# Five small experts in four 32-column tiles, and a large one as 128 and 32 rows

## The chip, the cores and the metric

The kernel runs on one core of a Trainium2 chip. The metric is the device time of one execution in microseconds (us), taken as the median of several runs. A profiled execution of the same program, a run by itself, gives the trace from which all rows below come; its span is counted from its first to its last instruction.

## What is computed

Three layers follow one another: an attention with a narrow window and block sums, a layer of eight experts of which each token takes one or none, and a dense feed-forward layer. The expert layer and the layer behind it are what matters here:

```python
skip_score = x @ w_skip                      # x: 1536 tokens of 512 numbers
do_compute = skip_score > 0
...
logits = xc @ w_gate                         # xc: the tokens to compute
e_idx = np.argmax(logits, axis=1)            # one of 8 experts
...
for e in range(E):
    mask = e_idx == e
    h = np.maximum(xc[mask] @ w1[e], 0.0)    # w1[e]: 512 x 1024
    y[mask] = gate_w[mask, None] * (h @ w2[e])   # w2[e]: 1024 x 512
out[do_compute] = xc + y
...
h = x @ w_in                                 # feed-forward: 512 x 2048
g = np.where(pos, h, np.where(neg, 0.0, (h + beta) ** 2 / (4.0 * beta)))
return (g @ w_out)                           # 2048 x 512
```

All is float32. For the inputs drawn here 428 of the 1536 tokens go to an expert; the eight experts get 179, 131, 60, 23, 13, 10, 9 and 3 of them. Tokens that are skipped go straight to the feed-forward layer.

## The kernel before, in words

**Routing.** The attention is computed for 12 tiles of 128 tokens. Each tile's rows are scattered to a buffer in memory (`xf`), skipped tokens from the front and computed ones from the back, and the row numbers of each expert's tokens go into a list (`ids_d`). The kernel does not know at build time which expert is large. It sorts the experts by counts on VectorE and works on eight places p = 0 to 7. Place 0 is the expert that is largest after three tiles; its first 128 tokens are computed at the end of the attention (`fb_x` to `fb_b`). Places 1 to NEARLY - 1 are experts that have gained few tokens of late, chosen after seven tiles. The rest are sorted at the end, largest first, and `PLACES` says which of them comes at which place.

**Experts.** `experts` runs over the places in the order 0 to 7. A place has room for 64 tokens, and the one in `BIG` (place 4) for 64 and another 128. The row numbers are loaded by SyncE (SP) in `get_ids`, and the rows gathered by GpSimd (POOL) in `get_x`, into one of 7 buffers x (`xring`) in turn, so that a gather waits for the scatter of the buffer's former rows. For a place of 64 rows, `x64` turns the rows (4 transposes of TensorE, PE), `a64` multiplies them with w1 in two halves of 512 columns, `t64` turns the result h (4 transposes), `b64` multiplies with w2, and `y64` adds the result to the rows on VectorE (DVE) and scatters them (`put`). In `a64` and `b64` the 64 tokens are the stationary operand, so each matmul fills only 64 of the 128 columns of PE; the two halves f = 0 and 1 write to PSUM partitions 0 to 63 and 64 to 127 and stand side by side. A float32 matmul is two instructions in the trace, so `a64` and `b64` are 16 each.

**Order.** PE, ACT and DVE instructions of the expert and feed-forward stages are ordered by a scheduler at build time, with priorities; SP and POOL follow the written order. At place p stand, in this order: `t64(p)`, `y64(p-1)`, `a64(p+1)`, the turning of place p+2, `b64(p)`. Weights of a place are 4 MB in four transfers of 1 MB (`fetch(p, c)`, c = 0, 1 for w1 and 2, 3 for w2), into slots that place p shares with p+3: `fetch(p+3, 0)` waits until `a64(p)` has ended, `fetch(p+3, 2)` until `b64(p)` has. Behind the last of them SP issues two reads of rows for the feed-forward layer (`get_slots` 0 and 1), the raw weights of its steps f = 4 and 5 (2 MB), and two more reads of rows (2 and 3).

**Feed-forward.** `feed` takes 512 tokens at a time (ch = 0 to 2) and 16 steps f of 128 columns each. Its weights come as 64-bit raw data that DVE and ACT rebuild into two float32 parts (`ff_bits` in three steps, `ff_round`); the steps f = 0 to 3 and the turning of the first 512 tokens (`turn0`) are filled into the expert stage, so many at each point as `FILLS` says. The first matmul of a step is `mm1` (tile hf). In the order of PE the first `mm1` stands behind the last expert's `b64` and all of `turn0`.

Of the kernel before, what the change touches and what calls it, by code (L numbers as in the profile page):

```python
# [8 lines left out]
F32 = mybir.dt.float32  # L9
# [4 lines left out]
ALU = mybir.AluOpType  # L14
# [8 lines left out]
SENT = 1 << 20  # L23
EARLY = 512
NV = 6
NEARLY = 3
BIG = (4,)
EOFF = 28 * CAP
SLOTS = (("00", "01"), ("02", "03"), ("10", "11"))
FFSLOTS = ("12", "13", "10", "11", "00", "01", "02", "03")  # L30
NRAW = 4
FILLS = ((2, 1, 1), (2, 1, 1), (2, 1, 1), (2, 1, 1), (0, 0, 0, 0), (0, 0, 0), (2, 0, 0))
LAST = 2
FFILLS = ((2, 1, 2), (2, 0, 2))
SHIFT = {'bits': 6, 'round': -57, 'act': -1, 'add': -97, 'g': 8, 'y': 18, 'x': -8, 't': 6, 'turn': 0}
YLAST = 4
PLACES = {3: 2, 4: 0, 5: 3, 6: 1, 7: 4}


@with_exitstack  # L40
def tile_net(ctx, tc, q, k, v, w_skip, w_gate, w1, w2, w_in, w_out, out):
    nc = tc.nc
    w_in, w_out = w_in.bitcast(I32), w_out.bitcast(I32)
    B, H, S, D = q.shape
    E = w_gate.shape[1]
# [22 lines left out]
    ident = cp.tile([128, 128], F32, name="ident")  # L68
# [35 lines left out]
    wx = {}  # L104
    ereg = {}

    def room(p):

        return 192 if p in BIG else 64

    def fetch(p, c):

# [33 lines left out]
    def rows(p, off):  # L146

        return ereg[p] * CAP + off + (ereg["n"] if p == 0 else 0)
# [22 lines left out]
    st = {}  # L171
# [9 lines left out]
    def get(key, row, n):  # L181

        get_ids(key, row, n)
        get_x(key)

    def get_ids(key, row, n):
        ids = cp.tile([128, 1], I32, tag="ids", name="ids", bufs=10)
        load_ids(ids[0:n], row)
        st["ids", key] = ids, n
# [36 lines left out]
    def attention(actx):  # L226
        per = actx.enter_context(tc.tile_pool(name="at_per", bufs=1))
        wk = actx.enter_context(tc.tile_pool(name="at_wk", bufs=2))
        rt = actx.enter_context(tc.tile_pool(name="rt", bufs=2))
        ps = actx.enter_context(tc.tile_pool(name="at_ps", bufs=2, space=PSUM))  # L230
# [629 lines left out]
    def experts(mctx):  # L860
        st["wk"] = wk = mctx.enter_context(tc.tile_pool(name="mo_wk", bufs=2))
        st["ps"] = ps = mctx.enter_context(tc.tile_pool(name="mo_ps", bufs=2, space=PSUM))

        def put(key, n):
            ids, xg = st.pop(("x", key))
            apart(scatter(ids[0:n], xg[0:n]), xg)


        def x64(key):
            xg = st["x", key][1]  # L870
            tp = ps.tile([128, 4, 64], F32, tag="tp", name="tpx", bufs=3)
            for kk in range(4):
                nc.tensor.transpose(tp[:, kk], xg[0:64, 128 * kk:128 * kk + 128], ident[0:64, 0:64])
            st["xT", key] = xT = wk.tile([128, 4, 64], F32, tag="xT", name="xT", bufs=3)
            with shift("x"):
                nc.scalar.copy(out=xT, in_=tp)  # L876

        def a64(key, p):
            xT = st["xT", key]
# [5 lines left out]
            st["h", key] = h = wk.tile([128, 512], F32, tag="h", name="h", bufs=2)  # L885
            nc.scalar.activation(out=h, in_=hp, func=AF.Relu)

        def t64(key):
            tp = turned(st.pop(("h", key)), ps.tile([128, 4, 128], F32, tag="tp", name="tph", bufs=3))
            st["hT", key] = hT = wk.tile([128, 4, 128], F32, tag="hT", name="hT", bufs=3)  # L890
            with shift("t"):
                nc.scalar.copy(out=hT, in_=tp)  # L892

        def b64(key, p):
            hT = st.pop(("hT", key))
# [7 lines left out]
        def y64(key):  # L903
            xg = st["x", key][1]
            yp = st.pop(("y", key))
            with shift("y"):
                for a in (0, 64):
                    nc.vector.scalar_tensor_tensor(out=xg[0:64, 0:512], in0=yp[a:a + 64], scalar=xg[0:64, 512:513],  # L908
                                                   in1=xg[0:64, 0:512], op0=ALU.mult, op1=ALU.add)
            put(key, 64)  # L910

        def mx(key):
            st["xT", key] = xT = wk.tile([128, 4, 128], F32, tag="xT", name="xTm", bufs=3)
            nc.scalar.copy(out=xT, in_=turned(st["x", key][1], ps.tile([128, 4, 128], F32, tag="tp", name="tpx", bufs=3)))

        def ma(key, p, f):
            if f == 0:
                t = wk.tile([128, 1024], F32, tag="h", name="hm")
                st["h", key] = t[:, 0:512], t[:, 512:1024]
            a128(p, st["xT", key], st["h", key], ps.tile([128, 512], F32, tag="h", name="hp", bufs=3), f)  # L920

        def mt(key):
            st["hT", key] = hT = wk.tile([128, 8, 128], F32, tag="hT", name="hTm", bufs=3)
            h = st.pop(("h", key))
            for a in range(2):
                t128(h, hT, ps.tile([128, 4, 128], F32, tag="tp", name="tph", bufs=3), a)

        def mb(key, p):
# [22 lines left out]
        x64(0)  # L951
        a64(0, 0)
        fetch(3, 0), fetch(3, 1)
        x64(1)
        st.pop("beyond")()
        for p in more:
            for key, off, m in more[p]:
                get_ids(key, rows(key[0] if m == 128 else key, off), m)
        for p in range(E - 1):
            last = p + 2 == E  # L960
            t64(p)
            if p in BIG:
                mt((p, 1))
            if p:
                y64(p - 1)
                if p - 1 in BIG:
                    put((p - 1, 1), 128)
            for key, off, m in more.get(p, ()):
                get_x(key)
            n = iter(FILLS[p])  # L970
            fill(next(n))
            a64(p + 1, p + 1)
            fill(next(n))
            if p + 1 in BIG:
                for f in range(2):
                    ma((p + 1, 1), p + 1, f)
            if p + 4 < E:
                fetch(p + 4, 0), fetch(p + 4, 1)
            for f in early[p]:
                f()  # L980
            if not last:
                x64(p + 2)
                if p + 2 in BIG:
                    mx((p + 2, 1))
            b64(p, p)
            if last:
                y64(p)
                t64(p + 1)
# [10 lines left out]
        b64(E - 1, E - 1)  # L999
        st["ylast"] = lambda: y64(E - 1)  # L1000
        fill(LAST)


# [294 lines left out]
```

## Time and profile before

| | us |
|---|---|
| median of 3 runs | 526.07 (525.96 to 526.61) |
| profiled execution, its time | 523.97 |
| profiled execution, its span | 521.9 |
| busy in the span: PE, DVE, ACT, POOL | 481.4, 271.6, 219.1, 94.7 |
| first instruction of the expert stage on PE | 149.88 |
| first `mm1` of the feed-forward stage | 241.10 |

The profiled execution is 2.1 us shorter than the median of the others, and its own time holds 2.1 us around the span. A difference found in the span is carried to the median as it stands. In the rows below, a line such as "160.07 3.65 PE L883 MATMUL hp<-w,xT ... x16" reads: at 160.07 us from the start of the span, for 3.65 us until the end of the last one, 16 matmuls of line 883 that write tile hp from tiles w and xT; "[1.67 <-ACT xh L205]" says that the engine stood idle for 1.67 us before it, until ACT's instruction of line 205 had ended. PEld is the loading of the stationary operand.

### The profile page before, as it was taken

What the parts mean: (1) busy time and instruction counts of PE and PEld (TensorE: products, weight loads), DVE (VectorE), ACT (ScalarE), POOL (GpSimd) and SP (SyncE); (2) the same over time, 40 slices, a digit from 0 to 9 for tenths busy, and PEclk for the clock granted to TensorE, in tenths of its full rate; (3) what the DMA queues carried; (4) which work ended last, traced back from release to release, by engine and by line L of the source; (5) the groups of instructions that cost most, each with busy time, mean ns of one, the idle gap of its engine ahead of it and who ended that gap; (6) DMA issues with size and microseconds to landing.
All of it is one profiled execution on the core that took longest, in us unless ns stands there. A gap on an engine that the chain in (4) does not pass through costs nothing.

```text
span 521.9 us, 7327 instructions
## 1 busy us (share of the span) xinstructions
PE 481.4 (92%) x2614; PEld 350.9 (67%) x2614; DVE 271.6 (52%) x612; ACT 219.1 (42%) x430; POOL 94.7 (18%) x167
## 2 busy tenths in 40 slices
PE   6887989973969999998999999999999999999994
PEld 3676979962423333435788888888888888888883
DVE  6665686972363421139899953433434453333341
ACT  6475637640112212122877666533324342333341
POOL 8505514505250310104000000020000011000002
PEclk9898989995879999998999999999999999999999
DMA  8997999989958999583654800020000001000002
GB/s 207 238 215 162 191 127 225 217 256 353 349 167 276 396 385 396 179 326 100 214 182 162 306 1 0 24 80 1 0 1 1 0 21 60 1 1 1 0 0 87
DMA packets 67981, 77.10 MB, mean 148 GB/s; under 512 B 32270, under 2 KB 49710, under 8 KB 67552
## 3 DMA queue, kind: packets, MB, share of 16 engines
q1 hardware_dynamic: 64480, 68.29, 45.7%
q0 software_dynamic: 3456, 8.26, 4.5%
q8 instruction: 22, 0.36, 0.3%
q14 instruction: 23, 0.19, 0.1%
HBM read 69.85 MB, written 8.12 MB: 149 GB/s over the span
## 4 chain that ended last, share of the span: by engine, by line
PE 45%; issue 34%; DVE 8%; ACT 5%; DMA 5%; POOL 1%; POOLq 0%; DVEq 0%; ACTq 0%
PE hf L1078 8%; PE hp L883 6%; PE yp L900 6%; DMA ids_d<-slot,si 3%; PE o L1119 3%; PE s L387 3%; PE o L1121 3%; PE o L1120 3%; PE hp L210 2%; PE lp L445 2%; PE xo L416 1%; POOL out_dram L1131 1%; PE yp L221 1%; DMA x<-xf,ids 1%; ACT p L392 1%
## 5 line engine op out<-in xcount | busy, mean ns | idle before, releaser
L1078 PE MATMUL hf<-xh,ffw 128*128 128x512 f32 x384 | 128.3, 396 | 1.7 <-ACT xh L205 1.7
L1078 PEld LDWEIGHTS hf<-xh,ffw 128*128 128x128 f32 x384 | 72.7, 189 | 18.3 <-ACT xh L205 1.9
L1119 PE MATMUL o<-ffw,g 128*128 128x512 f32 x192 | 76.8, 400 | 1.1 <-ACT g L1103 1.1
L1078 PE MATMUL hf<-xl,ffw 128*128 128x512 f32 x192 | 75.6, 394 | 0.4 <-DVE xl L206 0.4
L1120 PE MATMUL o<-ffw,g 128*128 128x512 f32 x192 | 75.9, 395 | 0.0
L1121 PE MATMUL o<-ffw,g 128*128 128x512 f32 x192 | 75.1, 395 | 0.0
L1131 POOL DMA_INDIRECT out_dram<-ob,perm x12 | 11.7, 974 | 257.5 <-DVE ob L1130 165.1
L1088 ACT ACTIVATE c<-c,scal 128x512 f32<-128x512 f32 x32 | 23.2, 724 | 76.7 <-DVE c L1087 76.6
L1098 DVE TENSOR_TENSOR hf<-hf,c 128x512 f32<-128x512 f32 x48 | 33.5, 698 | 41.1 <-ACT hf L1096 37.4
L1104 DVE TENSOR_TENSOR g<-hf,g 128x512 fp32r<-128x512 f32 x48 | 33.1, 689 | 24.6 <-ACT g L1103 24.6
L1087 DVE TENSOR_SCALAR c<-hf 128x512 f32<-128x512 f32 x32 | 22.1, 691 | 42.6 <-PE hf L1078 42.6
L1078 PEld LDWEIGHTS hf<-xl,ffw 128*128 128x128 f32 x192 | 36.5, 190 | 9.2 <-DVE xl L206 0.8
L1119 PEld LDWEIGHTS o<-ffw,g 128*128 128x128 f32 x192 | 36.1, 188 | 9.4 <-ACT g L1103 1.5
L1121 PEld LDWEIGHTS o<-ffw,g 128*128 128x128 f32 x192 | 36.2, 189 | 8.6
L1120 PEld LDWEIGHTS o<-ffw,g 128*128 128x128 f32 x192 | 36.3, 189 | 8.0
L392 ACT ACTIVATE p<-s,nm 128x120 f32<-128x120 f32 x96 | 26.7, 361 | 31.6 <-DVE nm L389 21.4
L1103 ACT CAST g<-hf 128x512 fp32r<-128x512 f32 x48 | 28.1, 586 | 28.1 <-DVE hf L1098 28.0
L883 PE MATMUL hp<-w,xT 128*64 128x512 f32 x128 | 32.0, 646 | 1.2 <-ACT xT L876 1.2
L908 DVE SCALAR_TENSOR_TENSOR x<-yp,x 64x512 f32<-64x512 f32 x16 | 12.0, 748 | 40.6 <-PE yp L900 33.0
L900 PE MATMUL yp<-w,hT 128*64 128x512 f32 x128 | 30.2, 599 | 0.7 <-ACT hT L892 0.7
L387 PE MATMUL s<-pb 128*128 128x120 f32 x192 | 27.3, 287 | 3.0 <-ACT pb L357 1.8
L387 PEld LDWEIGHTS s<-pb 128*128 128x128 f32 x192 | 27.2, 203 | 4.2 <-ACT pb L357 1.9
(203 smaller groups left out, 689.3 us busy)
## 6 DMA issues: line engine op xcount, KB each, us to landing
w<-in_moe_w_dram SPq DMA_DIRECT2D x32, 1024.0 KB, 10.9
raw<-in_moe_w_in_dram SPq DMA_DIRECT2D x16, 512.0 KB, 7.1
raw<-in_moe_w_out_dram SPq DMA_DIRECT2D x16, 512.0 KB, 4.6
x<-xf SPq DMA_DIRECT2D x12, 264.0 KB, 5.7
raw<-in_k_dram SPq DMA_DIRECT2D x16, 192.0 KB
raw<-in_q_dram SPq DMA_DIRECT2D x16, 192.0 KB, 4.4
vraw<-in_v_dram SPq DMA_DIRECT2D x4, 768.0 KB, 6.8
vw<-in_v_dram SPq DMA_DIRECT2D x13, 192.0 KB, 5.7
```

Of the source, the lines that this page charges most:

```text
L387: nc.tensor.matmul(s[:, u], tq[:, j], tk[:, j], start=False, stop=u == 3)
L392: nc.scalar.activation(out=p[:, u], in_=s[:, u], func=AF.Exp, bias=nm[:, u:u + 1], scale=1.0)
L883: nc.tensor.matmul(hp[64 * f:64 * f + 64], xT[:, kk], wx[p, 0][:, kk, 512 * f:512 * f + 512], start=kk == 0, stop=kk == 3)
L900: nc.tensor.matmul(yp[a], hT[:, kk, a], wx[p, 1][:, 4 * f + kk], start=kk == 0, stop=kk == 3)
L1078: nc.tensor.matmul(hp, w[:, 128 * kk:128 * kk + 128], a[:, kk], start=(n == 0), stop=(n == 11))
L1088: nc.scalar.activation(out=c, in_=c, func=AF.Square, bias=half, scale=0.5)
L1098: nc.vector.tensor_tensor(out=hp, in0=hp, in1=c, op=ALU.add)
L1103: nc.scalar.copy(out=gh, in_=hp)
L1104: nc.vector.tensor_tensor(out=gl, in0=hp, in1=gh.bitcast(F32), op=ALU.subtract)
L1119: nc.tensor.matmul(ops[ch][t], gh[:, a], hi, start=(f == 0), stop=False)
L1120: nc.tensor.matmul(ops[ch][t], gh[:, a], lo, start=False, stop=False)
L1121: nc.tensor.matmul(ops[ch][t], gl[:, a], hi, start=False, stop=(f == NF - 1))
```

## The change

Every place has a room of its own now: 64 rows at places 0 and 6, 32 rows at places 1, 2, 3, 5 and 7, and 160 at place 4, as 128 and 32. A place of n rows uses 128 / n tiles of n columns side by side (`sides`): for 32 rows four tiles, each with 256 columns of w1 in `as_`, and a quarter of w2's rows in `bs`; so h of 32 rows is 128 x 256, and two transposes turn it. `ys` adds the parts one by one: four additions for 32 rows, where 64 rows take two. One place more (3) is chosen early. Of the large expert, the part of 128 rows is gathered first and the part of 32 rows later; before, the part of 64 came first and that of 128 later.

```diff
-NEARLY = 3
+NEARLY = 4
 BIG = (4,)
+ROOM = (64, 32, 32, 32, 160, 32, 64, 32)
-FILLS = ((2, 1, 1), (2, 1, 1), (2, 1, 1), (2, 1, 1), (0, 0, 0, 0), (0, 0, 0), (2, 0, 0))
+FILLS = ((2, 1, 1), (1, 1, 0), (1, 1, 0), (1, 2, 1), (1, 1, 1, 1), (0, 0, 0), (2, 0, 0))
-PLACES = {3: 2, 4: 0, 5: 3, 6: 1, 7: 4}
+PLACES = {4: 0, 5: 2, 6: 1, 7: 3}
...
+    def tail(p):
+
+        return (128, ROOM[p] - 128) if p in BIG else (0, ROOM[p])
...
         for p in range(NEARLY):
-            get(p, rows(p, 0), 64)
+            get(p, rows(p, 0), room(p))
         late_regs()
-        get(3, rows(3, 0), 64)
         fb_b()
         fetch(2, 2), fetch(2, 3)
-        get(4, rows(4, 0), 64)
+        get((4, 1), rows(4, 0), 128)
...
+        def sides(n):
+
+            return [slice(n * i, n * i + n) for i in range(128 // n)]
...
-            hp = ps.tile([128, 512], F32, tag="h", name="hp", bufs=3)
+            n = st["n", key]
+            xT, m = st["xT", key], 8 * n
+            hp = ps.tile([128, m], F32, tag="h", name="hp", bufs=3)
             for kk in range(4):
-                for f in range(2):
-                    nc.tensor.matmul(hp[64 * f:64 * f + 64], xT[:, kk], wx[p, 0][:, kk, 512 * f:512 * f + 512],
-                                     start=kk == 0, stop=kk == 3)
+                for f, a in enumerate(sides(n)):
+                    nc.tensor.matmul(hp[a], xT[:, kk], wx[p, 0][:, kk, m * f:m * f + m], start=kk == 0, stop=kk == 3)
...
-            for kk in range(4):
-                for f in range(2):
-                    a = slice(64 * f, 64 * f + 64)
-                    nc.tensor.matmul(yp[a], hT[:, kk, a], wx[p, 1][:, 4 * f + kk], start=kk == 0, stop=kk == 3)
+            for c in range(n // 16):
+                for f, a in enumerate(sides(n)):
+                    nc.tensor.matmul(yp[a], hT[:, c, a], wx[p, 1][:, n // 16 * f + c], start=c == 0, stop=c == n // 16 - 1)
...
-                for a in (0, 64):
-                    nc.vector.scalar_tensor_tensor(out=xg[0:64, 0:512], in0=yp[a:a + 64], scalar=xg[0:64, 512:513],
-                                                   in1=xg[0:64, 0:512], op0=ALU.mult, op1=ALU.add)
-            put(key, 64)
+                for a in sides(n):
+                    nc.vector.scalar_tensor_tensor(out=xg[0:n, 0:512], in0=yp[a], scalar=xg[0:n, 512:513],
+                                                   in1=xg[0:n, 0:512], op0=ALU.mult, op1=ALU.add)
+            put(key, n)
...
-        more = {0: (((4, 1), 64, 128), (5, 0, 64)), 1: ((6, 0, 64),), 3: ((7, 0, 64),)}
+        more = {0: (4, 5), 1: (6,), 3: (7,)}
```

On PE, from the transposes of place 2 to those of place 4, before (x_71 and x_72 hold the rows of places 2 and 3, x_73 and x_74 the two parts of place 4; the order counts a float32 matmul once):

```order
L873 MATMUL tpx<-ident,x_71 128x64 x4
L900 MATMUL yp<-w_1372,hT 64x512 x8
L200 MATMUL tph<-ident,h 128x128 x4
L883 MATMUL hp<-w_1938,xT 64x512 x8
L873 MATMUL tpx<-ident,x_72 128x64 x4
L900 MATMUL yp<-w_1899,hT 64x512 x8
L200 MATMUL tph<-ident,h 128x128 x4
L883 MATMUL hp<-w_2215,xT 64x512 x8
L873 MATMUL tpx<-ident,x_73 128x64 x4
L200 MATMUL tpx<-ident,x_74 128x128 x4
L900 MATMUL yp<-w_2176,hT 64x512 x8
```

and the same stretch of PE now:

```order
L881 MATMUL tpx<-ident,x_71 128x32 x4
L910 MATMUL yp<-w_1372,hT 64x512 x8
L900 MATMUL tph<-ident,h 128x128 x2
L892 MATMUL hp<-w_1948,xT 32x256 x16
L881 MATMUL tpx<-ident,x_72 128x32 x4
L910 MATMUL yp<-w_1909,hT 32x512 x8
L900 MATMUL tph<-ident,h 128x128 x2
L892 MATMUL hp<-w_2215,xT 32x256 x16
L881 MATMUL tpx<-ident,x_74 128x32 x4
L205 MATMUL tpx<-ident,x_73 128x128 x4
L910 MATMUL yp<-w_2176,hT 32x512 x8
```

The steps stand in the same order; only their shapes and counts differ, and the small part of place 4 is still turned ahead of the 128 rows, though it lies in the other buffer now.

On POOL, the gathers from the fourth on, before (xf<-x_73 is the scatter of the first 128 tokens, xf<-x_76 that of place 0):

```order
L163 DMA x_72<-xf,ids 64x528
L168 DMA xf<-x_73,ids_1654 1536x528
L163 DMA x_73<-xf,ids 64x528
L163 DMA x_74<-xf,ids 128x528
L163 DMA x_75<-xf,ids 64x528
L168 DMA xf<-x_76,ids 1536x528
```

and now:

```order
L168 DMA x_72<-xf,ids 32x528
L173 DMA xf<-x_73,ids_1654 1536x528
L168 DMA x_73<-xf,ids 128x528
L168 DMA x_74<-xf,ids 32x528
L168 DMA x_75<-xf,ids 32x528
L173 DMA xf<-x_76,ids 1536x528
```

The 128 rows of place 4 have taken the fifth place, and its small part the sixth.

## Rows read from the trace of the kernel before

**Rows 1.** The page: span, and busy time of each engine.

```profile
span 521.9 us, 7327 instructions
PE 481.4 (92%) x2614; PEld 350.9 (67%) x2614; DVE 271.6 (52%) x612; ACT 219.1 (42%) x430; POOL 94.7 (18%) x167
```

**Rows 2.** Timeline of PE, 100 to 250 us: one place, the large one, the end.

```profile
160.07 3.65 PE L883 MATMUL hp<-w,xT 128*64 128x512 f32 x16
163.66 0.46 PE L873 MATMUL tpx<-ident,x 64*128 64x64 f32 x4
164.04 3.65 PE L900 MATMUL yp<-w,hT 128*64 128x512 f32 x16
167.63 0.66 PE L200 MATMUL tph<-ident,h 128*128 128x128 f32 x4
168.22 3.65 PE L883 MATMUL hp<-w,xT 128*64 128x512 f32 x16
...
179.95 0.46 PE L873 MATMUL tpx<-ident,x 64*128 64x64 f32 x4
...
208.73 7.13 PE L221 MATMUL yp<-w,hTm 128*128 128x512 f32 x16
...
234.75 3.65 PE L900 MATMUL yp<-w,hT 128*64 128x512 f32 x16 [0.67 <-ACT hT L892]
238.34 1.09 PE L200 MATMUL tps<-ident,x 128*128 128x128 f32 x8
241.10 0.96 PE L1078 MATMUL hf<-xh,ffw 128*128 128x512 f32 x3 [1.67 <-ACT xh L205]
```

**Rows 3.** Waits of PE from 160 to 239 us (total, times, longest).

```profile
PE yp L900 <- ACT hT L892: 0.7, 1, 0.7
```

**Rows 4.** Windows: busy of each engine, granted clock, DMA share, GB/s.

```profile
160.00:210.00 50.00, 50.00 (x229) 18.82 (x228) 15.65 (x18) 11.87 (x22) 8.12 (x9) 1.00 1.03 380
210.00:222.00 12.00, 12.00 (x48) 4.81 (x48) 1.13 (x2) 1.45 (x3) 1.90 (x2) 1.00 0.53 161
222.00:232.00 10.00, 10.00 (x50) 3.79 (x48) 2.81 (x6) 2.26 (x4) 0.91 (x1) 1.00 1.05 385
232.00:234.00 2.00, 2.00 (x10) 0.69 (x6) 0.75 (x2) 0.00 (x0) 0.00 (x0) 1.00 0.44 161
```

**Rows 5.** Timeline of SP, 215 to 240 us: the last weights and the rows.

```profile
215.90 0.95 SPq L118 DMA_DIRECT2D w<-in_moe_w_dram  x2
...
225.26 1.90 SPq L852 DMA_DIRECT2D x<-xf  x2
```

**Rows 6.** Single weight transfers issued at 168.57 and 195.84 us, to landing.

```profile
w<-in_moe_w_dram SPq DMA_DIRECT2D x1, 1024.0 KB, 11.3
w<-in_moe_w_dram SPq DMA_DIRECT2D x1, 1024.0 KB, 8.7
```

**Rows 7.** Timeline of PEld near 104 us: stationary loads of 64 columns, attention.

```profile
103.59 0.60 PEld L416 LDWEIGHTS xo<-pb,pts 120*64 120x64 f32 x16
```

**Rows 8.** Timeline of POOL, 142 to 246 us: the sixth gather of expert rows.

```profile
169.50 1.03 POOL L163 DMA_INDIRECT x<-xf,ids  x1 [9.11 <-DMA ids<-ids_d]
```

**Rows 9.** Its issue: KB (none known), us to landing.

```profile
x<-xf,ids POOLq DMA_INDIRECT x1, 6.5
```

**Rows 10.** Timeline of ACT ahead of the first `mm1`.

```profile
239.03 0.58 ACT L205 CAST xh<-tps 128x512 fp32r<-128x512 f32 x1 [4.33 <-PE tps L200]
239.51 1.05 ACT L1043 CAST ffw<-cv 128x1024 fp32r<-128x1024 f32 x1
240.46 0.59 ACT L205 CAST xh<-tps 128x512 fp32r<-128x512 f32 x1
```

**Rows 11.** Instructions on tile yp: DVE's additions (ns, least, median, most).

```profile
L908 DVE SCALAR_TENSOR_TENSOR x<-yp,x x16: 742/748/753, 167.7 to 242.5; 64x512 f32<-64x512 f32 x16
L222 DVE SCALAR_TENSOR_TENSOR x<-yp,x x2: 732/742/751, 147.7 to 215.9; 128x512 f32<-128x512 f32 x2
```

**Rows 12.** Windows of the feed-forward stage, columns as in rows 4.

```profile
243.00:247.00 4.00, 4.00 (x12) 3.12 (x12) 4.00 (x5) 0.11 (x1) 3.52 (x1) 0.57 0.02 6
260.00:300.00 40.00, 40.00 (x175) 32.54 (x174) 38.29 (x48) 28.61 (x42) 0.00 (x0) 1.00 0.63 222
```

More of the change, by code (lines that the diff above doesn't have):

```diff
@@ L107, in room @@
     def room(p):
-        return 192 if p in BIG else 64
+        return ROOM[p]
+    def tail(p):
+        return (128, ROOM[p] - 128) if p in BIG else (0, ROOM[p])
     def fetch(p, c):
@@ L188, in get_ids @@
         load_ids(ids[0:n], row)
-        st["ids", key] = ids, n
+        st["ids", key], st["n", key] = (ids, n), n
     def get_x(key):
@@ L866, in put, with xs @@
             apart(scatter(ids[0:n], xg[0:n]), xg)
-        def x64(key):
-            xg = st["x", key][1]
-            tp = ps.tile([128, 4, 64], F32, tag="tp", name="tpx", bufs=3)
+        def sides(n):
+            return [slice(n * i, n * i + n) for i in range(128 // n)]
+        def xs(key):
+            n, xg = st["n", key], st["x", key][1]
+            tp = ps.tile([128, 4, n], F32, tag="tp", name="tpx", bufs=3)
             for kk in range(4):
-                nc.tensor.transpose(tp[:, kk], xg[0:64, 128 * kk:128 * kk + 128], ident[0:64, 0:64])
-            st["xT", key] = xT = wk.tile([128, 4, 64], F32, tag="xT", name="xT", bufs=3)
+                nc.tensor.transpose(tp[:, kk], xg[0:n, 128 * kk:128 * kk + 128], ident[0:n, 0:n])
+            st["xT", key] = xT = wk.tile([128, 4, n], F32, tag="xT", name="xT", bufs=3)
@@ L875, in x64, with as_ @@
             with shift("x"):
                 nc.scalar.copy(out=xT, in_=tp)
-        def a64(key, p):
-            xT = st["xT", key]
-            hp = ps.tile([128, 512], F32, tag="h", name="hp", bufs=3)
+        def as_(key, p):
+            n = st["n", key]
+            xT, m = st["xT", key], 8 * n
+            hp = ps.tile([128, m], F32, tag="h", name="hp", bufs=3)
             for kk in range(4):
-                for f in range(2):
-                    nc.tensor.matmul(hp[64 * f:64 * f + 64], xT[:, kk], wx[p, 0][:, kk, 512 * f:512 * f + 512],
-                                     start=kk == 0, stop=kk == 3)
-            st["h", key] = h = wk.tile([128, 512], F32, tag="h", name="h", bufs=2)
+                for f, a in enumerate(sides(n)):
+                    nc.tensor.matmul(hp[a], xT[:, kk], wx[p, 0][:, kk, m * f:m * f + m], start=kk == 0, stop=kk == 3)
+            st["h", key] = h = wk.tile([128, m], F32, tag="h", name="h", bufs=2)
@@ L886, in a64, with ts @@
             nc.scalar.activation(out=h, in_=hp, func=AF.Relu)
-        def t64(key):
-            tp = turned(st.pop(("h", key)), ps.tile([128, 4, 128], F32, tag="tp", name="tph", bufs=3))
-            st["hT", key] = hT = wk.tile([128, 4, 128], F32, tag="hT", name="hT", bufs=3)
+        def ts(key):
+            h, n = st.pop(("h", key)), st["n", key] // 16
+            tp = ps.tile([128, n, 128], F32, tag="tp", name="tph", bufs=3)
+            for c in range(n):
+                nc.tensor.transpose(tp[:, c], h[:, 128 * c:128 * c + 128], ident)
+            st["hT", key] = hT = wk.tile([128, n, 128], F32, tag="hT", name="hT", bufs=3)
@@ L891, in t64, with bs @@
             with shift("t"):
                 nc.scalar.copy(out=hT, in_=tp)
-        def b64(key, p):
-            hT = st.pop(("hT", key))
+        def bs(key, p):
+            hT, n = st.pop(("hT", key)), st["n", key]
             yp = ps.tile([128, 512], F32, tag="y", name="yp")
-            for kk in range(4):
-                for f in range(2):
-                    a = slice(64 * f, 64 * f + 64)
-                    nc.tensor.matmul(yp[a], hT[:, kk, a], wx[p, 1][:, 4 * f + kk], start=kk == 0, stop=kk == 3)
+            for c in range(n // 16):
+                for f, a in enumerate(sides(n)):
+                    nc.tensor.matmul(yp[a], hT[:, c, a], wx[p, 1][:, n // 16 * f + c], start=c == 0, stop=c == n // 16 - 1)
@@ L901, in b64, with ys @@
             st["y", key] = yp
[L903 to L904 removed]
+        def ys(key):
+            xg, n = st["x", key][1], st["n", key]
             yp = st.pop(("y", key))
             with shift("y"):
[L907 to L910 removed]
+                for a in sides(n):
+                    nc.vector.scalar_tensor_tensor(out=xg[0:n, 0:512], in0=yp[a], scalar=xg[0:n, 512:513],
+                                                   in1=xg[0:n, 0:512], op0=ALU.mult, op1=ALU.add)
+            put(key, n)
@@ L949, in experts @@
             early[5 + c // 2].append(lambda c=c: get_slot(c))
-        x64(0)
-        a64(0, 0)
+        xs(0)
+        as_(0, 0)
         fetch(3, 0), fetch(3, 1)
-        x64(1)
+        xs(1)
         st.pop("beyond")()
         for p in more:
-            for key, off, m in more[p]:
-                get_ids(key, rows(key[0] if m == 128 else key, off), m)
+            for o in more[p]:
+                get_ids(o, rows(o, tail(o)[0]), tail(o)[1])
         for p in range(E - 1):
             last = p + 2 == E
-            t64(p)
+            ts(p)
             if p in BIG:
@@ L964, in experts @@
             if p:
-                y64(p - 1)
+                ys(p - 1)
                 if p - 1 in BIG:
                     put((p - 1, 1), 128)
-            for key, off, m in more.get(p, ()):
-                get_x(key)
+            for o in more.get(p, ()):
+                get_x(o)
             n = iter(FILLS[p])
             fill(next(n))
-            a64(p + 1, p + 1)
+            as_(p + 1, p + 1)
             fill(next(n))
@@ L981, in experts @@
             if not last:
-                x64(p + 2)
+                xs(p + 2)
                 if p + 2 in BIG:
                     mx((p + 2, 1))
-            b64(p, p)
+            bs(p, p)
             if last:
-                y64(p)
-                t64(p + 1)
+                ys(p)
+                ts(p + 1)
             fill(next(n))
@@ L998, in experts @@
                 ff_fetch(NRAW), ff_fetch(NRAW + 1)
-        b64(E - 1, E - 1)
-        st["ylast"] = lambda: y64(E - 1)
+        bs(E - 1, E - 1)
+        st["ylast"] = lambda: ys(E - 1)
         fill(LAST)
```

## The prediction

> **What bounds the kernel now.** The page first: PE is busy for 481.4 of 521.9 us [rows 1], no other engine for more than half as long as the span is. PE is thus the engine to look at, but its busy time is a mean over stages, and the change touches one stage. So the timeline of PE comes next. A place takes 8.15 us there (one first half starts at 160.07, the next at 168.22): 3.59 for the first half, 0.38 for the transposes of x, 3.59 for the second half, 0.59 for those of h [rows 2], counted from start to start. The waits say that PE stood idle for 0.7 us only between 160 and 239 us [rows 3]. So the expert stage is bound by PE, from start to end.
>
> The windows then show a second resource that is just as full. From 160 to 210 us the DMA engines are busy all the time (share 1.03) at 380 GB/s, which is 19.0 MB, 18 transfers of weights. Only behind that does the share fall, to 0.53 between 210 and 222 us, and it is full again until about 232.9 (0.44 of the last two us) [rows 4]. The gap has a cause that can be read: the last two weights of place 7 go out at 215.90 [rows 5], when place 4's second half of 128 rows, which frees their slot, has run on PE (208.73 and 7.13 us) [rows 2]. The reader is to see that the stage has two full resources, PE without a gap and DMA with a gap of 12 x (1 - 0.53) = 5.6 us. What is taken from PE pays only until DMA has become the bound.
>
> **The change part by part.** *Work of PE.* Six keys shrink from 64 to 32 rows: five places and the small part of place 4. Per key the first half is 32 instructions of 256 columns instead of 16 of 512; the second stays at 16 of 512, four side by side instead of two. How four tiles run the trace doesn't show. Bounds: 16 instructions of 128 columns, which stand alone, take 7.13 us; 16 of 64 columns take 3.59 [rows 2], so two tiles run fully side by side. Four, run as fully, give 1.8 per half; if only two of the four ever overlap, 3.6; if none, 7.1. I take 1.8, since the step from one tile to two is lossless. The loads of the stationary operand don't forbid it: 16 loads of 64 columns go through in 0.60 us [rows 7], so 32 loads of half the width need at most 1.2. Two transposes of h fall away, 0.3 us. A key thus costs 8.15 - 2 x 1.8 - 0.3, about 4.25, and six keys save 6 x 3.9 = 23.4 us of PE.
>
> *The new order of gathers.* The small part of place 4 is now the sixth gather on POOL. That gather goes out at 169.50, after 9.11 us of waiting for its row numbers [rows 8], which SP can only ask for behind the first two transfers of place 3; it lands 6.5 us later [rows 9], at 176.0. Neither moves, because the first half of place 0, for which those transfers wait, keeps its 64 rows. PE turned the small part at 179.95 [rows 2]; four halves and two turnings earlier, 7.2 + 0.6 less and about 0.2 for smaller transposes, it would come there at 172. So PE waits about 4 us, a new wait. Behind it in PE's queue stand the second half of place 2 and both first halves of place 4, and those wait with it; DVE has nothing urgent. I count 2 us more for a clock that falls in the pause: the granted clock was 0.57 between 243 and 247 us [rows 12], the lower of the two levels (1.2 and 2.4 GHz) for most of it, after PE had waited 1.67 us for ACT [rows 2].
>
> *PE's end by itself.* The last second half ended at 238.3; less 23.4, plus 4 and 2: 221.
>
> *The transfers.* Weights from place 3 on are 20 transfers. The sixth was issued at 168.57 and landed 11.3 us later, the fifteenth at 195.84 and 8.7 later [rows 6]: 179.9 and 204.5, 2.74 us each. The pace was DMA's own, and the change takes no byte of weights away. At this pace the tenth (second half of place 4) lands at 190.9, the eighteenth (place 6) at 212.8, the twentieth (place 7) at 218.3. PE ended place 4's 128 rows at 215.9 [rows 2]; nine smaller halves and four smaller turnings come before that, 17.4 us, and 6 us of pause and clock go against them: 204.5, ahead of 210, when the queue ran dry [rows 4]. So the gap of 5.6 us closes. Behind the twentieth the same transfers follow as before: rows, 2 MB of raw weights, rows. All of it ended at 232.9; without the gap, at 227.3. This is later than PE's own end of 221, so the reads of rows 2 and 3, the last in the queue, are late next: their transposes, and behind them the first `mm1`, stand in PE's order after everything else.
>
> *From there to the first `mm1`.* Before, 2.76 us lay between the transposes (238.34) and `mm1` (241.10) [rows 2], of which a rounding of weights, 1.05, stood between ACT's two copies [rows 10]; the built order has it ahead of both now. With 1.8 and 0.4 for transposes on a slow clock, `mm1` starts at 229.5 instead of 241.1: 11.6 us earlier.
>
> *Additions on DVE.* One addition takes 748 ns for 64 partitions and 742 for 128 [rows 11], so for 32 it takes as long, and four of them 3.0 us where two took 1.5: 9 us more over six keys. In the expert stage DVE is busy for 15.65 of 50 us [rows 4], and this covers them; it would cost up to 1.5 us per key without the cover. Only place 7's stand where the cover is thin: in the built order all four precede the feed-forward's first addition. I take the full 1.5 (bounds 0 and 1.5).
>
> *At no cost:* an early choice more (one register load on SP more before, one less after), `FILLS` (the same 20 pieces of work, later, while DVE has room), and smaller gathers (empty places in a list move no rows that anyone waits for). The feed-forward stage itself keeps its instructions. PE has no gap there from 260 to 300 us, with DVE at 38.29 of 40 [rows 12], so an earlier start is kept to the end if DVE's work starts earlier by as much; its raw weights do, as they lie in the same queue of transfers.
>
> **The sum.** 11.6 - 1.5 = 10.1 us off the span of 521.9: 511.8, or 513.9 in the profiled execution's own time (523.97). The median of the runs lies 2.1 higher, at 526.07; there the sum gives 516.0.
>
> **The rivals.** *Four tiles run no faster than two.* Nothing in the trace shows four. Then only transposes are saved, 6 x 0.4 = 2.4 us of PE, the gather lands before PE needs it, and the time is about 524. It decides from a half of 2.4 us on: then PE's end moves from 221 by 12 x 0.6 to 228, level with DMA. Against it: two tiles lost nothing.
>
> *The transfers don't close up.* If SP, which issues in order, or a slot holds a transfer back, or the feed-forward's start stalls on DVE with its raw weights in hand later than I think, part of the gain is lost: half of the gap and of the earlier end, some 5 us, 521. For it: SP waits at each fetch for PE, and PE gets a new pause of 4 us; against it: at 172 us some ten transfers of weights have been issued, so the pause starves nothing.
>
> *PE alone is the bound.* If the reads of rows overtake the raw weights, `mm1` would start at 221 + 2.2 and the gain be 16 us: 510. Against it: SP issues them in order [rows 5], and the transfers before them were served so [rows 6].
>
> *Slower: four tiles side by side cost more than two*, in `as_` and `bs`, because the instructions pass one after another. A half would take 7.1 instead of 3.59, a key 2 x 3.5 - 0.3 = 6.7 more, and six keys 40 us on a stage where PE has no slack: 566. It decides where a half takes more than 3.8, which eats the saved transposes. Against it: loads and matmuls of two tiles interleave within 0.60 us [rows 7].
>
> *The additions become the bound.* Rows first: 32 partitions take as long as 128 [rows 11]; if each key's extra 1.5 us stood on the path (the buffer of yp is freed later, and the second half after next waits), 6 x 1.5 = 9 of the 11.6 us would be lost and the time be 523.5. It needs DVE to be later than PE at each place, where 3.0 us stand against a key's 4.25; with the conversions of the feed-forward between them that can be so at one or two places, not at six. The Trainium skill states this as a rule against such a change: tiling speeds up TensorE but not the emptying of PSUM, which may become the bottleneck after a fourfold speed-up (TensorEngine Tiling (Array Packing), Performance Considerations, PSUM Bottleneck). By that rule the time would be the 523.5 of this rival. The trace agrees that the additions don't shrink with the rows.
>
> **How the numbers follow.** Forecast, 10.1 us off: 0.66. Closing up only in part: 0.13. Two tiles at a time: 0.08, additions as the bound: 0.04. PE alone: 0.05. Slower: 0.04. The predicted time is 516.0 us. Its own range, from the 1.5 us of additions, 2 us of clock and the landing pace (2.74 against 2.65 to 2.85 for twenty transfers), is 513 to 519. To leave out no more than 2 in 10 the range goes on to the partial case: 512 to 522. The two rivals of little gain, 0.12 together, may end within 0.2% (1.05 us, about what a measurement of this kernel can tell from no change) for a third of that, and slower for a tenth: faster 0.91, same 0.04, slower 0.05.
>
> **What would show it.** Right: a half of 32 rows in about 1.8 us; a pause of PE near 172 to 176 us ahead of place 4's transposes; a DMA share of 1.0 without a gap from 160 to 227; the first `mm1` near 229.5, waiting for rows 2 and 3; the distance from there to the end unchanged at 281 us, give or take 1.5. Wrong: halves of 3.6 us, a gap in the transfers before 220, or an `mm1` that starts early and a feed-forward stage that is longer by as much.

## The result, and the profile after

| | before | after |
|---|---|---|
| median of 4 runs each, us | 526.02 (525.44 to 526.61) | 515.12 (514.52 to 516.89) |
| ratio, 95% interval | | 0.9846 (0.9802 to 0.9889) |
| profiled execution: time, span | 523.97, 521.9 | 514.87, 513.2 |
| first half of place 0 starts | 152.37 | 155.40 |
| first `mm1` starts | 241.10 | 231.41 |

The forecast was 516.0, within 512 to 522. The ratio leaves out executions in a slower state of the chip and is not the quotient of the two medians: 0.9846 of 526.02 is 8.1 us less, the medians differ by 10.9 us, and the spans of the two profiled executions by 8.7. The page after, first lines (span; then busy time and share of each engine):

```profile
span 513.2 us, 7501 instructions
...
PE 464.8 (91%) x2698; PEld 348.3 (68%) x2698; DVE 279.9 (55%) x624; ACT 217.4 (42%) x430; POOL 89.2 (17%) x167
```

PE is busy for 16.6 us less than in [rows 1], and the span is 8.7 us shorter. Where PE works and where it waits is seen in its timeline of the changed kernel (start, duration, work, and in brackets the idle time ahead of it and what ended that):

```profile
153.65 0.66 PE L881 MATMUL tpx<-ident,x 64*128 64x64 f32 x4 [9.62 <-DMA x<-xf,ids]
...
155.40 7.26 PE L892 MATMUL hp<-w,xT 128*64 128x512 f32 x26
...
168.92 1.93 PE L892 MATMUL hp<-w,xT 128*32 128x256 f32 x32
...
171.14 1.92 PE L910 MATMUL yp<-w,hT 128*32 128x512 f32 x16
...
173.36 1.93 PE L892 MATMUL hp<-w,xT 128*32 128x256 f32 x32
...
176.07 0.40 PE L881 MATMUL tpx<-ident,x 32*128 32x32 f32 x4 [0.78 <-DMA x<-xf,ids]
...
221.82 1.67 PE L205 MATMUL tps<-ident,x 128*128 128x128 f32 x8 [2.78 <-DMA x<-xf]
...
228.89 1.85 PE L205 MATMUL tps<-ident,x 128*128 128x128 f32 x8 [1.98 <-DMA x<-xf]
231.41 1.65 PE L1088 MATMUL hf<-xh,ffw 128*128 128x512 f32 x3 [0.68 <-ACT xh L210]
...
244.31 0.51 PE L1129 MATMUL o<-ffw,g 128*128 128x512 f32 x1 [2.30 <-ACT g L1113]
```

Three things are to be seen. A half of 32 rows takes 1.93 us, where one of 64 took 3.59 [rows 2], and a key 4.44 (168.92 to 173.36) instead of 8.15. At the end PE waits where it never waited before [rows 3]: 2.78 and 1.98 us for rows of the last stage (`tps`, line 205; rows 0 and 1 first, then rows 2 and 3). And the stage begins 3 us later: PE is idle for 9.62 us ahead of place 0. The windows (busy time of each engine, granted clock, share of the DMA engines, GB/s) show what it waits for at the end:

```profile
160.00:210.00 50.00, 48.58 (x348) 19.24 (x344) 22.53 (x27) 11.63 (x26) 9.25 (x10) 0.99 0.98 364
210.00:222.00 12.00, 9.22 (x70) 3.91 (x67) 4.62 (x7) 1.25 (x3) 1.80 (x2) 1.00 1.05 389
```

The share between 210 and 222 us is 1.05 where it was 0.53 [rows 4]: the gap in the transfers is closed.

**How the executions are compared.** The experiments ran on chips where one kernel's runs spread over 5 to 10 us (the kernel before 523.0 to 529.4 in one set, 530.5 to 535.5 in another), and ahead of the expert stage the executions already differ by more: the first gather goes out between 145.9 and 157.6 us. So each set has its ratio to the kernel before, and an expectation in us, written for a kernel before of 526 us, is held against the ratio. Small effects are read from three distances in the profiled execution: A from the issue of the first gather (POOL) to the start of place 0's first half, B from there to the first `mm1`, C from there to the end of the span. The kernel before has one trace, so how far its three distances repeat is not known. Worked out from the rows of each trace (us):

```
kernel                         gather  first half    mm1     span      A       B       C
before                         145.88    152.37    241.10   521.9    6.49   88.73   280.8
the change                     146.81    155.40    231.41   513.2    8.59   76.01   281.8
the change, second time        151.05    159.69    236.77   519.9    8.64   77.08   283.1
the change, third time         146.84    155.80    232.23   515.1    8.96   76.43   282.9
two tiles                      155.10    164.57    252.55   533.3    9.47   87.98   280.8
tiles alone                    157.63    166.35    243.30   525.9    8.72   76.95   282.6
fetch later                    156.45    161.83    239.25   522.2    5.38   77.42   283.0
rows first                     157.10    165.68    238.82   517.4    8.58   73.14   278.6
two additions                  148.59    157.61    233.63   517.6    9.02   76.02   284.0
1 MB less                      149.11    157.98    231.24   513.2    8.87   73.26   282.0
less work of PE                147.41    156.44    232.35   511.3    9.03   75.91   279.0
fetch later and rows first     151.96    157.80    231.48   510.8    5.84   73.68   279.3
all three                      149.66    154.67    229.35   508.6    5.01   74.68   279.3
old fillings                   148.64    157.83    234.15   517.5    9.19   76.32   283.4
```

### The profile page after: what moved, and what is told of

Same layout as the page of the kernel before. It is cut to its first block, busy times and chain, and to the rows that moved or that the text cites. A ratio compares the mean times of both kernels' runs of the same rounds, so it can differ in the third digit from the quotient of the medians.

```text
span 513.2 us, 7501 instructions
## 1 busy us (share of the span) xinstructions
PE 464.8 (91%) x2698; PEld 348.3 (68%) x2698; DVE 279.9 (55%) x624; ACT 217.4 (42%) x430; POOL 89.2 (17%) x167
## 4 chain that ended last, share of the span: by engine, by line
PE 36%; issue 35%; DMA 13%; DVE 6%; ACT 4%; SPq 3%; POOL 1%; POOLq 0%; ACTq 0%; DVEq 0%
PE hf L1088 9%; DMA x<-xf,ids 4%; PE s L392 3%; DMA ids_d<-slot,si 3%; DMA ids<-ids_d 3%; PE o L1129 3%; PE o L1131 3%; PE o L1130 3%; PE hp L215 2%; PE xo L421 2%; DMA x<-xf 2%; PE hp L892 2%; PE lp L450 2%; PE yp L226 1%; POOL out_dram L1141 1%
## 5 line engine op out<-in xcount | busy, mean ns | idle before, releaser
L918 DVE SCALAR_TENSOR_TENSOR x<-yp,x 32x512 f32<-32x512 f32 (+1 forms) x28 | 20.8, 744 | 28.6 <-PE yp L910 21.6
L1053 ACT CAST ffw<-cv 128x1024 fp32r<-128x1024 f32 x16 | 16.6, 1040 | 18.2 <-DVE cv L1038 6.9
L892 PE MATMUL hp<-w,xT 128*32 128x256 f32 (+1 forms) x224 | 23.3, 440 | 0.0
```

Of the source, the lines that this page charges most:

```text
L892: nc.tensor.matmul(hp[a], xT[:, kk], wx[p, 0][:, kk, m * f:m * f + m], start=kk == 0, stop=kk == 3)
```

## The experiments

**First set** (the kernel before: 532.52 us, 530.54 to 535.54).

*Two tiles.*

```diff
-ROOM = (64, 32, 32, 32, 160, 32, 64, 32)
+ROOM = (64, 64, 64, 64, 192, 64, 64, 64)
```

> All of the change but the 32 columns: every expert of few tokens gets 64 rows again (two 64-column tiles side by side), the late large one 128 and 64. Choice of the three early experts, order of the two parts and the table of fillings stay changed. Theory (the tiles carry the gain): a half of a key goes back from 1.93 to 3.59 us, six keys cost some 23 us of TensorE more, of which the new pauses at the end (2.78, 1.98 and 0.78 us) hide about 6; with the stage's start still 3 us later than before, the time is 526 to 530 us, no faster than before. Rival (choice, order and fillings carry the gain): 518 us or less.

534.72 us, ratio 1.0039 (1.0010 to 1.0068): a little slower than before, as the theory has it (1.0039 of 526 is 528). B is 87.98, as before's, and A as long as the change's. Without the 32 columns nothing of the gain is left. A is 2.98 us longer than before, B 0.75 shorter and C the same, 2.2 us in all, and 0.39% of 532.52 is 2.1: so the earlier start of the kernel before, which one trace shows, is seen in the time too.

*Tiles alone.* The rows and the four tiles stay; the choice, the order of the parts and the fillings go back.

```diff
-NEARLY = 4
+NEARLY = 3
...
-PLACES = {4: 0, 5: 2, 6: 1, 7: 3}
+PLACES = {3: 2, 4: 0, 5: 3, 6: 1, 7: 4}
...
         late_regs()
+        get(3, rows(3, 0), room(3))
         fb_b()
         fetch(2, 2), fetch(2, 3)
-        get((4, 1), rows(4, 0), 128)
+        get(4, rows(4, 0), tail(4)[1])
...
```

> Only the 32 rows and their four tiles; choice of two early experts, order of the large one's parts (small one first) and table of fillings as before. Theory (tiles carry the gain, and the 3 us later start comes from the weight transfers that now go out beside the first gathers): the stage starts at 149.9 as before, the first matmul of the last stage at about 228.5, and the time is 511 to 513 us, faster than the full change. Rival (the choice and the order are needed for the gain): 517 us or more.

528.01 us, ratio 0.9883 (0.9830 to 0.9936). By the time the theory is missed and the rival's number met: 0.9883 of 526 is 520, where the rival said 517 or more. But its reason does not hold: B is the change's (76.95), so the tiles alone carry the stage. What is missing is the early start: A is 8.72, so the old order did not bring it back. The weight transfers go out 0.9 us behind the first gather here (158.56 and 157.63), where before they were 3.1 behind it (148.97 and 145.88), and PE waits 4.39 us for the rows of the second gather.

*Fetch later.* A one-element write by GpSimd, behind the first four gathers, holds back the last two weight transfers of place 2. The index load of place 4's 128 rows moves ahead of them, and its gather behind `fb_b`.

```diff
     def fetch(p, c):
...
+        if (p, c) == (2, 2):
+            nc.gpsimd.memset(wx[p, 1][0:1, 0, 0:1], 0.0)
...
         late_regs()
+        get_ids((4, 1), rows(4, 0), 128)
-        fb_b()
         fetch(2, 2), fetch(2, 3)
-        get((4, 1), rows(4, 0), 128)
+        fb_b()
+        get_x((4, 1))
```

> The whole change, but the last two weight transfers of place 2 wait for a one-element write that GpSimd does after it has issued the first four gathers; they go out at about 152 instead of 146.8. Theory (their 2 MB took the first gather's share of the DMA engines): the first gather lands within 4.5 us instead of 6.7, the first small expert starts about 3 us earlier, so do the transfers of place 3 and all behind them, and the time is 511 to 513.5 us. Rival 1 (the gather is late for another reason, such as its own later issue): start unmoved, 514 to 516. Rival 2 (start moves, but the delayed transfers end the stage at the same time): start 2 us or more earlier, and still 514 to 516.

524.79 us, ratio 0.9847 (0.9800 to 0.9895), which is the ratio of the change: the time shows no gain, against the theory. The trace shows the start: A is 5.38 instead of 8.59 to 8.96. PE's timeline shows what came in exchange:

```profile
160.11 0.43 PE L884 MATMUL tpx<-ident,x 64*128 64x64 f32 x4 [4.21 <-DMA x<-xf,ids]
...
185.81 0.60 PE L884 MATMUL tpx<-ident,x 32*128 32x32 f32 x4 [4.03 <-DMA x<-xf,ids]
```

The pause ahead of place 4's small part is 4.03 us now, and B is 0.3 to 1.4 us longer than in the change's three executions. Of some 3.4 us won in A 2 to 3 remain at the first `mm1`, and the medians of this set cannot tell that from nothing.

*Rows first.*

```diff
-            early[5 + c // 2].append(lambda c=c: get_slot(c))
+            early[5].append(lambda c=c: get_slot(c))
```

> The whole change, but SyncE issues the reads of rows 2 and 3 of the last stage ahead of the four transfers of feed-forward weights 4 and 5. Theory (transfers bound the stage, and these two reads end it): the waits of 2.78 and 1.98 us ahead of their transposes shrink below 1 us each, the first matmul of the last stage comes 3 to 5 us earlier (226.5 to 228.5), and the time is 510 to 513 us. Rival 1 (TensorE would be no earlier, or the weights 4 and 5 are missed in turn): 514 to 516 us, with a new wait for the conversion of those weights. Rival 2 (reads can't go earlier, since their buffers come free late): 514 to 516 with the two waits as they are.

519.33 us, ratio 0.9746 (0.9714 to 0.9778); the interval lies below that of the change (from 0.9802). The wait for rows 2 and 3 is gone and B falls to 73.14. The wait for rows 0 and 1, whose reads the edit does not move, is 2.85 us, where the theory had both below 1 us. C falls too, to 278.6. The windows around the first `mm1`, of this kernel:

```profile
239.00:242.00 3.00, 3.00 (x13) 2.24 (x14) 2.97 (x5) 0.00 (x0) 0.00 (x0) 1.00 0.00 0
242.00:245.00 3.00, 3.00 (x15) 2.48 (x14) 2.94 (x5) 2.47 (x4) 0.00 (x0) 1.00 0.38 89
```

and of the change:

```profile
231.00:234.00 3.00, 2.59 (x6) 1.78 (x7) 2.94 (x5) 0.36 (x1) 0.00 (x0) 0.50 0.74 286
234.00:237.00 3.00, 3.00 (x11) 2.40 (x10) 2.97 (x4) 0.00 (x0) 1.23 (x1) 0.69 0.00 0
```

The granted clock is 1.00 there and was 0.50 and 0.69 (0.50 is the lower of the two levels, 1.2 and 2.4 GHz) behind PE's waits for rows. Six us at those clocks are 3 x 0.50 + 3 x 0.31 = 2.4 us of work at full clock, most of the 3.2 us by which C differs. The rest is in PE's wait for ACT ahead of the first `o`, the second product of the feed-forward stage (line 1129): 2.30 us in the change, 1.36 here.

**Second set** (before: 528.22, 523.2 to 533.1).

*The change, second time.* No edit.

> The whole change once more, unaltered, as the measure for the three beside it on this chip. Theory: 0.985 of the kernel before, with the same waits near the end of the expert stage (rows of the last stage twice, 2 to 3 us each) and a first small expert that starts some 10 us after the last matmul of the large expert's first part. Rival (the late start was an accident of one execution): it starts 6 us after it, as before.

519.20 us, ratio 0.9805 (0.9734 to 0.9876). PE waits 11.82 us ahead of place 0, and A is 8.64: the late start of the changed kernel is no accident of one execution.

*Two additions.*

```diff
             with shift("y"):
-                for a in sides(n):
+                for a in sides(n)[0:2]:
```

> The whole change, but each key of few tokens adds only two of its four partial results (output of those tokens is incomplete). Theory (VectorE's work at the end of the stage costs what lies behind the first matmul of the last stage): 0.5 to 1.5 us less than the whole change on the same chip. Rival (VectorE's additions are all hidden): no difference within 0.3 us. Second rival (the additions hold up the scatters and so bound the stage): 4 us or more less.

520.08 us, ratio 0.9825 (0.9737 to 0.9913), no gain beside the change's 0.9805. B is unmoved and C, at 284.0, no shorter. My own theory (0.5 to 1.5 us) does not show, and the rival that they bound the stage (4 us or more) falls. That the extra additions are wholly hidden is not shown either: the interval is nearly 1% wide to either side, and C of the change alone goes from 281.8 to 283.1.

*1 MB less.*

```diff
     def fetch(p, c):
...
+        if (p, c) == (E - 1, 3):
+            return
...
-                    nc.tensor.matmul(yp[a], hT[:, c, a], wx[p, 1][:, n // 16 * f + c], start=c == 0, stop=c == n // 16 - 1)
+                    nc.tensor.matmul(yp[a], hT[:, c, a], wx[p, 1][:, (n // 16 * f + c) % (4 if p == E - 1 else 8)], start=c == 0, stop=c == n // 16 - 1)
```

> The whole change, but the last weight transfer of place 7 (1 MB) is left out; its matmuls read the half that is there. Theory (the stream of transfers bounds the end of the stage): the rows of the last stage land some 2.7 us earlier, and the time is 2 to 3 us less than the whole change on the same chip. Rival (TensorE bounds it): less than 0.5 us.

513.80 us, ratio 0.9719 (0.9654 to 0.9784). The median is 5.4 us below the change's, more than either theory gives, in a set that spreads by as much; B, the distance in which a transfer can act, is 73.26, 2.8 to 3.8 below the change's three. A transfer is 2.74 us by [rows 6]: the stream of transfers sets the end of the stage.

*Less work of PE.*

```diff
-            for kk in range(4):
+            last = 1 if p > 4 else 3
+            for kk in range(last + 1):
...
-            for c in range(n // 16):
+            last = n // 32 - 1 if p > 4 else n // 16 - 1
+            for c in range(last + 1):
...
```

> The whole change, but places 5 to 7 do half of the matmuls of either half (the same output tiles, half of the contraction; some 8 us of TensorE less, all bytes still loaded). Theory (the stream of transfers bounds the end of the stage): the waits for rows grow by what TensorE saves, and the time falls by less than 2 us (what little lies behind the last row: half of place 7's second half, 1 us, and what place 5 frees earlier). Rival (TensorE bounds it): 5 to 8 us less.

514.81 us, ratio 0.9761 (0.9686 to 0.9836). In the stage it went by the theory: B is 75.91, 0.1 to 1.2 below the change's, although PE did some 7.4 us less (half of two halves of 3.59 and of four of 1.93). It waits for weights and rows instead:

```profile
212.43 1.04 PE L912 MATMUL yp<-w,hT 128*64 128x512 f32 x2 [0.96 <-DMA w<-in_moe_w_dram]
215.66 3.33 PE L912 MATMUL yp<-w,hT 128*64 128x512 f32 x6 [2.19 <-DMA w<-in_moe_w_dram]
221.97 1.94 PE L205 MATMUL tps<-ident,x 128*128 128x128 f32 x8 [2.99 <-DMA x<-xf]
...
229.16 1.94 PE L205 MATMUL tps<-ident,x 128*128 128x128 f32 x8 [2.35 <-DMA x<-xf]
```

But the time fell by 4.4 us, between the two predictions, which I had not expected. Of that, C gives 2.8 to 4.1, behind the stage: PE does not wait ahead of the first `o` at all, and the clock is below 1.00 for a shorter time. Why is not isolated.

**Third set** (before: 527.31, 522.99 to 529.42).

*The change, third time.* No edit.

> The whole change, unaltered, as the measure for the three beside it: 0.978 to 0.987 of the kernel before.

518.90 us, ratio 0.9865 (0.9792 to 0.9938).

*Fetch later and rows first.* Both edits of the first set.

> The whole change with both edits to the queue: place 2's last two weight transfers behind the first four gathers, and the reads of rows 2 and 3 ahead of the feed-forward weights 4 and 5. Theory (one edit moves the start of the transfers, the other what ends them, so they add up in part): the pause of some 4 us ahead of place 4's small part stays, and the time is 5 to 9 us less than the whole change. Rival (the early start is lost in the stage, as the pause grows): 3 to 5 us less, no more than the rows alone give.

510.08 us, ratio 0.9668 (0.9607 to 0.9730), 8.8 us below the change. A is 5.84, B 73.68, C 279.3: the two edits keep what each showed in the trace. The pause at place 4 is 3.12 us.

*All three.* The index loads of places 4 to 7 go ahead of place 2's held transfers as well.

```diff
         get_ids((4, 1), rows(4, 0), 128)
+        for o in (4, 5, 6, 7):
+            get_ids(o, rows(o, tail(o)[0]), tail(o)[1])
         fetch(2, 2), fetch(2, 3)
...
-        for p in more:
-            for o in more[p]:
-                get_ids(o, rows(o, tail(o)[0]), tail(o)[1])
```

> As the run beside it, and the index loads of the late places go out before any further weight transfer, so that the gathers of place 4's small part and of place 5 start some 10 us earlier. Theory (that gather is late because its indices land behind the weights of place 3): the pause ahead of place 4's small part goes, and the time is 1 to 4 us less than with the two edits, 7 to 12 us less than the whole change. Rival (transfers bound the stage whatever TensorE waits for there): the pause goes and the time stays within 1 us of the two edits.

510.01 us, ratio 0.9670 (0.9606 to 0.9734). The pause is gone, as its rows show (no wait in front of line 886):

```profile
172.07 1.93 PE L897 MATMUL hp<-w,xT 128*32 128x256 f32 x32
173.93 0.43 PE L886 MATMUL tpx<-ident,x 32*128 32x32 f32 x4
```

The time is that of the two edits, and in the traces A and B together are 79.69 where they were 79.52. The rival holds: at this point transfers bound the stage, and PE's wait at place 4 costs nothing that shows. PE now waits further on: 1.18 and 1.58 us for weights of place 6 and 2.59 us for rows, where the run beside it has no such wait.

*Old fillings.*

```diff
-FILLS = ((2, 1, 1), (1, 1, 0), (1, 1, 0), (1, 2, 1), (1, 1, 1, 1), (0, 0, 0), (2, 0, 0))
+FILLS = ((2, 1, 1), (2, 1, 1), (2, 1, 1), (2, 1, 1), (0, 0, 0, 0), (0, 0, 0), (2, 0, 0))
```

> The whole change with the old table of fillings, which puts the conversions of the first feed-forward weights into the first four places. Theory (VectorE and ScalarE wait a third of the stage, so the place of the fillings costs nothing): within 1.5 us of the whole change. Rival (the table was needed because the keys have become shorter): 3 us or more slower, with waits of TensorE for ScalarE's copies in places 1 to 3.

519.28 us, ratio 0.9850 (0.9780 to 0.9920), 0.4 from the change, and B is 76.32: no cost of the table shows.

## Why the prediction was right, and where it was not

**The sum closes, with one term missing.** Predicted: 11.6 us up to the first `mm1`, -1.5 behind it, 10.1 off the span. Measured in the profiled executions: the start 3.03 us later (missing), B 12.72 shorter, C 1.0 longer: 8.7. From the median before, 8.7 us would have led to 517.3; that the forecast lies 0.9 us from the measured median is luck in part, since the medians differ by 2.2 us more than the spans, and no term explains that.

**Work of PE: right.** 1.93 and 1.92 for a half against the 1.8 taken, 4.44 for a key against 4.25. Sixteen instructions in four tiles side by side take 1.92 us, where sixteen that stand alone take 7.13 [rows 2]: 3.7 times as fast. PE's busy time fell by 16.6 us, where six keys at 8.15 less 4.44 make 22.3; but it differs by 5.9 us between executions with the same work of PE (481.4 before, 487.3 with two tiles), so the rows of the keys are the better measure. (DVE was busy for 271.6 of 521.9 us, a little over half the span and not less, as the prediction has it; nothing rests on that.) The rivals of two tiles and of slower tiles fall by these rows; that the tiles carry the gain is shown by taking them away (1.0039). For three column tiles of 32 columns the Trainium skill lists a speed-up of 2.38 (TensorE: Matmul & The Clock Gate, Part 3: Packing small matmuls — row/col tiling); no run here has three.

**Transfers as the bound: right, and shown from both sides.** The gap closed (0.53 to 1.05), 1 MB less shortens B by 2.8 to 3.8 us, some 7.4 us of PE less shorten it by at most 1.2. With them falls the rival that PE alone is the bound. The 20 transfers and what follows went as priced: B was forecast at 229.5 - 152.4 = 77.1 and is 76.0. Only the rows 2 and 3 were forecast to be late; the rows 0 and 1 are late too (2.78 us).

**"Neither moves": wrong.** The step took the first half of place 0 to start as before because its 64 rows stay, and it starts 3.03 us later. Place 2's last two transfers, 2 MB, now go out beside the first gather and no longer 3.1 us behind it. What moved them is not shown. SP issues four index loads ahead of them in either kernel; before, the fourth stood behind the register loads of the late places and went out at 148.16, now it stands ahead of them, and they are one fewer. But with that order back ("tiles alone") the transfers still went out 0.9 us behind the first gather. These are the issues of POOL and of SP after:

```profile
146.81 0.99 POOL L168 DMA_INDIRECT x<-xf,ids  x1 [12.71 <-DMA ids<-ids_d]
```

```profile
146.78 0.99 SPq L123 DMA_DIRECT2D w<-in_moe_w_dram  x2
```

Holding the transfers back takes A from 8.6 to 9.5 us, in all ten runs of the changed kernel and its variants without that edit, to 5.0 to 5.8 in the three with it. The landings say the same. In the kernel before, the first two gathers land 3.9 and 2.6 us after their issue, and the third and fourth, issued behind the transfers, 6.4 us each; in the changed kernel the first two take 6.7 each; in "all three", with the transfers held, 3.5 and 2.4. So contention with the gathers is shown. The Trainium skill says that transfers issued by POOL and by SP run on the same DMA engines and interleave (DMA: Bandwidth & Descriptors, Issuing engines are not separate DMA queues), and that each of these engines takes turns between its queues (the same page, Queues, rings and completion order); by that rule the gather shares its engines with the 2 MB, and the trace agrees. Of the 3.03 us, 2.1 are A's; the other 0.9 is the gather's own later issue, which differs by more than that between executions of the same kernel and stays open.

**The pause of 4 us at place 4: mis-sized, for the same reason.** It was 0.78, since PE came 3 us later; where the start is early again it is 4.03 and 3.12. That it hides behind the transfers was right: without it the time is the same (510.01 against 510.08).

**Additions: near in size, but not shown as the cause.** C grew by 1.0 against the 1.5 taken. But half of the additions left out gives nothing back that could be read. What C goes with is what PE loses in the first 24 us behind the first `mm1`: idle time, and time at a granted clock below 1.00. (The loss is 24 us less the sum of busy time times clock, in steps of 0.5 us.) It is 3.2 us before, 4.5, 5.5 and 5.4 in the change's three, 1.4 with rows first and 1.6 with less work of PE; C less this loss is 277.2 to 277.9 in thirteen of the fourteen executions, and 279.1 with two additions. From before to after the clock takes 0.5 us more (2.2 against 1.7) and idle time 0.8 more (2.3 against 1.5). The idle time is in the wait for g, the operand that ACT and DVE prepare, ahead of the first `o`, 2.30 us after (line 1129 above) and 1.06 before:

```profile
252.96 0.51 PE L1119 MATMUL o<-ffw,g 128*128 128x512 f32 x1 [1.06 <-ACT g L1103]
```

The low clock follows PE's waits for rows; that they cause it is not proven, since the run with the rows first moves both. One addition of 32 rows takes 0.74 us, as [rows 11] let expect. The Trainium skill's warning that emptying PSUM may become the bottleneck after a fourfold speed-up (TensorEngine Tiling (Array Packing), Performance Considerations, PSUM Bottleneck) is not borne out here: the two-additions run was no faster (0.9825 against 0.9805).

**At no cost: none seen.** The old fillings make 0.4 us, which is within the spread, and without the early choice B is the same (76.95).

## What to carry to other kernels

When one engine is relieved, cost the next bound in the same stage: here some 22 us of TensorE's work bought 12.7, because the transfers filled up. Then look at what is queued last on the new bound: two reads of 128 rows moved ahead of four weight loads were worth about 1% more, with no work saved. And do not take the start of a stage as fixed because its own work is unchanged: read which transfers go out beside the one that it waits for.

## What the runs showed that was not expected

A gather of 64 rows that goes out beside 2 MB of weights costs its consumer some 3 us more (A 8.6 and above against 5.0 to 5.8). While the transfers bound the stage, a TensorE pause of 3.12 us did not show in the time (510.08 with it, 510.01 without). And an edit to the queue ahead of a dense stage paid twice: rows first won 3 us ahead of the first `mm1` (B) and 3 behind it (C), of which 2.2 go with the clock, 0.50 and 0.69 there in the change and 1.00 with rows first, and 0.9 with the wait for ACT's g.
